# Filter and mixer on one core: the first batch's filter output handed to the mixer within SBUF instead of by way of DRAM

## The chip, the cores and the metric

The kernel runs on one core of a Trainium2 chip. The metric is the device time of one execution in microseconds; the kernel before was timed in three runs. A profile is one execution recorded by the hardware profiler. TensorE (PE) multiplies matrices, VectorE (DVE) and ScalarE (ACT) work elementwise, GpSimd (POOL) does a few sums and issues DMAs, SyncE (SP) only issues DMAs. SBUF is the memory on the core, with 128 partitions; DRAM is the memory beside it.

## The reference, cut to what matters

```python
# x: (8, 3008, 256) f32; filters: (1505, 256) f32; the four mixer weights are float64
def _attn_ref(x, filt_r, filt_i):
    X = np.fft.rfft(x, axis=1)
    Y = X * (filt_r + 1j * filt_i)[None, :, :]
    return np.fft.irfft(Y, n=x.shape[1], axis=1).astype(np.float32)

def _moe_ref(x, w_tok1, w_tok2, w_ch1, w_ch2):
    xt = x.transpose(0, 2, 1)
    h = np.maximum(xt @ w_tok1, 0.0) @ w_tok2      # token mixing, 3008 -> 256 -> 3008
    u = x + h.transpose(0, 2, 1)
    h2 = np.maximum(u @ w_ch1, 0.0) @ w_ch2        # channel mixing, 256 -> 1536 -> 256
    return (u + h2).astype(np.float32)

def reference(**kwargs):
    ...                                            # attention arguments and moe_ arguments parted
    return _moe_ref(x=_attn_ref(**attn_kwargs), **moe_kwargs)
```

The Fourier transform of length 3008 = 47 x 64 is done as matrix products. Its first step runs over 64 points, its second over 47 for each of 32 residues k (`K2`), with the filter's product between; then the steps run backward. The last backward step is not done for itself: it is folded into the token weights (`w1` is turned by `wai_t`), so that the token sums take the results of the second step as they are. These are called g or t4 below. The row for residue k has 4 partitions, 4k to 4k+3, each with 24 values of `a` by 256 channels.

The mixer's weights come as float64. The kernel loads them as 64-bit words in tiles and turns each into a top and a rest in float32 on ScalarE and VectorE: "converting a tile". There are 12 tiles of `w_tok1` and 14 of `w_tok2`, then those of the channel weights. The `w_tok1` tiles and the first six of `w_tok2` also pass through TensorE.

## The kernel before

The main parts that the change and the steps below touch:

```python
BY_PE = 6          # tiles of w_tok2 that pass through TensorE
IN_B = 16          # tiles converted beside the second filter step of the first batch
PARTS = (0, 64, 96, 112)

    t4p = pool("t4p", A // TC4 + 1)                       # 7 buffers of [128, 4, 256] f32
    ...
    def filt_load(c, first):                              # filter rows of residues 2c, 2c + 1
        t, k0 = filts[c % FB], c * KC                     # FB = 3 buffers, KC = 2
        q = nc.gpsimd if first and c != 1 else nc.sync
        for src, i, p0 in (...):                          # first: filt_r and filt_i
            q.dma_start(t[p0:p0 + A, i], raw(src, k0, [[64 * D, A], [D, KC], [1, D]]))
            ...                                           # two more DMAs of mirrored rows
    def filt_double(c):
        nc.scalar.copy(out=t[HALF:P], in_=t[0:HALF])      # line 234
    ...
    def halves(st, n, pair):                              # converting, lines 262 to 270
        nc.scalar.activation(out=top, in_=hi_f, func=AF.Copy, scale=2.0 ** -112)
        yield
        nc.vector.tensor_scalar(...); nc.vector.scalar_tensor_tensor(...)
        yield
        nc.vector.tensor_scalar(...); nc.vector.scalar_tensor_tensor(...)
        yield top, rest
    ...
    def on_chip(stat, top, rest, n, parts):               # the tiles that pass through TensorE
            nc.tensor.matmul(ps[:, 0:n], stat, top, start=True, stop=False)     # line 303
            nc.tensor.matmul(ps[:, 0:n], stat, rest, start=False, stop=True)    # line 304
            for src, dst in parts:
                nc.scalar.copy(out=dst, in_=src(ps))      # line 306
    ...
    def b_unit(k):                                        # second step, forward, and filter
            nc.tensor.matmul(ps, wbs[...], t2, start=True, stop=True)           # line 535
            nc.vector.tensor_tensor(out=p1, in0=ps.to_broadcast([P, 2, D]),
                                    in1=t[:, :, k % KC, :], op=ALU.mult)        # line 543
    def bi_unit(k):                                       # second step, backward
            nc.tensor.matmul(ps[0:KR], wi, p, ...)        # line 560, two per residue
            nc.scalar.copy(out=t3s[c][:, r]..., in_=ps[0:KR]...)                # line 566
            if r == KC - 1:                               # every second residue
                nc.scalar.dma_start(g_d[b, ts(c, KC)]..., t3[:, :, i, :])       # line 571, to DRAM
    ...
    def t4_load(b, c, lo=PARTS[0], hi=P, queue=nc.sync):  # line 611, from DRAM
        queue.dma_start(t4[b, c][lo:hi], rows_of(g_d, b)[lo:hi, ts(c, TC4), :])
    def token_sums(b):                                    # line 617, 48 products
        for a in range(A):
            for t in range(TC):
                nc.tensor.matmul(acc[:, t, :], w1[:, a, ts(t, P)], t4[b, a // TC4][:, a % TC4, :], ...)
    ...
    # the first batch, residue by residue, with tiles converted beside it
                if k == K2 - 5:
                    pause.append(True)                    # begin no new tile loads
                while half < 2 * IN_B * (k + 1) // K2:
                    ...                                   # half a tile's conversion
                if 19 <= k < 25:
                    t4_load(0, k - 19, 0, PARTS[1])       # partitions 0 to 63 back from DRAM
                elif ...                                  # 64 to 95, 96 to 111
        for c in range(A // TC4):
            t4_load(0, c, PARTS[3], P, (nc.sync, nc.gpsimd)[c % 2])   # 112 to 127
        pause.clear()
        ...
        for i in range(IN_B, A // 2 + TC * W2G):          # tiles 16 to 25
            convert()
            if i == A // 2 + BY_PE - 1:                   # after tile 17
                sum_up()
                acc = token_sums(0)
```

The token sums need all of `w1` and all of t4 of the batch; the mixer behind them needs `w2` as well. The other seven batches run through the filter beside the mixer of the batches ahead of them, by way of DRAM.

Of the kernel before, what the change touches and what calls it, by code (L numbers as in the profile page):

```python
# [10 lines left out]
FP32 = mybir.dt.float32  # L11
I64 = mybir.dt.int64
# [7 lines left out]
N1 = 47  # L20
N2 = 64
NF = N // 2 + 1
D = 256
P = 128
K2 = 32
A = 24
# [4 lines left out]
TC4 = 4  # L31
# [3 lines left out]
KC = 2  # L35
WC = 2
DT = 256
TC = DT // P
# [3 lines left out]
DH = D // P  # L42
# [2 lines left out]
MT = 6  # L45
NG = 10
W2G = -(-N2 // NG)
PARTS = (0, 64, 96, 112)
BY_PE = 6
IN_B = 16  # L50
EARLY = 12
GROUPS = ((0,), (1, 2), (3, 4), (5, 6), (7,))

# [74 lines left out]
def kernel(  # L128
# [11 lines left out]
    nc = tc.nc  # L140
# [12 lines left out]
    g_d = nc.dram_tensor("g_tmp", (B, K2, KR, D), FP32, kind="Internal").ap()  # L153
# [3 lines left out]
    def pool(name, bufs, **kw):  # L157
        return ctx.enter_context(tc.tile_pool(name=name, bufs=bufs, **kw))

    glob = pool("glob", 1)  # L160
# [5 lines left out]
    p1p = pool("p1p", 2)  # L166
    p2p = pool("p2p", 1)
    t3p = pool("t3p", 2)
    t4p = pool("t4p", A // TC4 + 1)
    h1p = pool("h1p", 1)  # L170
    up = pool("up", 2)
    hp = pool("hp", 2)
# [21 lines left out]
    wai = glob.tile([P, P], FP32, name="wai")  # L194
# [4 lines left out]
    filts = [glob.tile([P, 2, KC, D], FP32, name="filt%d" % i) for i in range(FB)]  # L199
    w1 = glob.tile([P, A, DT], FP32, name="w1")  # L200

    w2 = glob.tile([P, TC, A * P], FP32, name="w2")

    w2m = [w2[:, t, 0:7 * 256].rearrange("p (s n) -> p s n", s=7) for t in range(2)]
# [8 lines left out]
    def raw(src, row, ap):  # L213
        return bass.AP(tensor=src.tensor, offset=src.offset + row * D, ap=ap)

    def filt_load(c, first):
        t, k0 = filts[c % FB], c * KC


        q = nc.gpsimd if first and c != 1 else nc.sync  # L220
        for src, i, p0 in ((filt_r, 0, 0), (filt_i, 1, 0 if first else HALF)) + (() if first else ((filt_r, 0, HALF),)):
            q.dma_start(t[p0:p0 + A, i], raw(src, k0, [[64 * D, A], [D, KC], [1, D]]))
            lo = p0 + 32
            if k0 == 0:
                q.dma_start(t[lo:lo + A, i, 0, :], raw(src, 32, [[64 * D, A], [1, D]]))
            k = max(k0, 1)

            for j0, n in ((0, 16), (16, A - 1 - 16)):
                q.dma_start(t[lo + j0:lo + j0 + n, i, k - k0:KC, :],
                            raw(src, 64 * (j0 + 1) - k, [[64 * D, n], [-D, k0 + KC - k], [1, D]]))  # L230
# [14 lines left out]

    early = [(up, "u")] * 2 + [(tp, "t")] * 2 + [(vp, "v")] * 2
    late = [(t2p, "t2"), (t3p, "t3")]
    stages = [(t4p, "t4")] * (A // 2) + (early * 3)[0:TC * W2G + DH] + late * 5

    def stage(n):  # L250
        where, tag = stages.pop(0)
        return where.tile([P, n], I64, tag=tag, name="st")

# [41 lines left out]
    ended = [0]  # L295
# [33 lines left out]
    def w2_load(i):  # L329

        t, g = divmod(i, W2G)
        nn = min(NG, N2 - g * NG)
        n = nn * N1

        more = g + 1 < W2G
        st = stage(512)
        nc.gpsimd.dma_start(st[:, 0:n + more], moe_w_tok2[ts(t, P), ds(g * NG * N1, n + more)])
        yield
        dst = w2[:, t].rearrange("p (a h n2) -> p h n2 a", h=2, n2=HALF)[:, :, ds(g * NG, nn), :]

        def some(h, nh, w):
            return (lambda v: bass.AP(tensor=v.tensor, offset=v.offset + h * A, ap=[v.ap[0], [A, nh], [N1, nn], [1, w]]),
                    dst[:, h:h + nh, :, 0:w])

        parts = [some(0, 2, A)] if more else [some(0, 1, A), some(1, 1, A - 1)]
        if i < BY_PE:
            h = halves(st, n + more, spare_pair())
            yield next(h)
            yield next(h)
            on_chip(ident, *next(h), n + more, parts)  # L350
        else:
            yield from rounded(st, n + more, parts, False)
# [23 lines left out]
    def wc2_load(i):  # L376
# [5 lines left out]
        def tile_of(dh):  # L382
# [7 lines left out]
    LAST = ((wc2_load, 0), (wc1_load, 1), (wc1_load, 4), (wc2_load, 1), (wc1_load, 2), (wc2_load, 2), (wc1_load, 5),  # L390
            (wc2_load, 3), (wc2_load, 4), (wc2_load, 5))

    tiles = ([w1_load(i) for i in range(A // 2)] + [w2_load(i) for i in range(TC * W2G)]
             + [wc1_load(c * (DC // 512), False) for c in range(DH)] + [f(i) for f, i in LAST])
# [7 lines left out]
    def sum_up():  # L402
        while behind:
            behind.pop(0)()
# [21 lines left out]
            advance(copy)  # L426
            copied[0] += 1

    begun, pause = [0], []

    def fill(ahead):
        while not pause and begun[0] < len(tiles) and begun[0] < ended[0] + (4 if begun[0] >= len(tiles) - len(LAST) else ahead):
            start()

    def start():
# [5 lines left out]
    xs, ahead = {}, []  # L441
# [22 lines left out]
    def rows_of(t_d, b):  # L464
        return t_d[b].rearrange("k (g a) d -> (k g) a d", a=A)
# [12 lines left out]
    def dft(bs):  # L478
        first = bs[0] == 0
# [40 lines left out]
        t2s, t3s, prods = {}, {}, {}  # L520
# [32 lines left out]
        def bi_unit(k):  # L553


            ps = bank(free_bank() if first else held.pop(0)).rearrange("p (b d) -> p b d", b=2)[:, 0:nb, :]
            parts = prods.pop(k)
            for i, p in enumerate(parts):
                wi = turn_i[:, k // WC % 4, k % WC] if i else wbs[k // WC][:, k % WC, P:]
                nc.tensor.matmul(ps[0:KR], wi, p, start=(i == 0), stop=(i == len(parts) - 1))  # L560
            c, r = divmod(k, KC)
            if r == 0:
                where, tag = (p2p, "p2") if first and c % 3 == 2 else (t3p, "t3")
                t3s[c] = where.tile([KR, KC, nb, D], FP32, tag=tag, name="t3")

            nc.scalar.copy(out=t3s[c][:, r].rearrange("p b (e g i) -> p b g e i", e=DH, i=CW),  # L566
                           in_=ps[0:KR].rearrange("p b (g e i) -> p b g e i", e=DH, i=CW))
            if r == KC - 1:
                t3 = t3s.pop(c)
                for i, b in enumerate(bs):  # L570
                    nc.scalar.dma_start(g_d[b, ts(c, KC)].rearrange("k r d -> r k d"), t3[:, :, i, :])
# [31 lines left out]

    t4 = {}

    def t4_load(b, c, lo=PARTS[0], hi=P, queue=nc.sync):
        if lo == 0:
            t4[b, c] = t4p.tile([P, TC4, D], FP32, tag="t4", name="t4")  # L610
        queue.dma_start(t4[b, c][lo:hi], rows_of(g_d, b)[lo:hi, ts(c, TC4), :])

    def token_sums(b):
        acc = bank(free_bank()).rearrange("p (t d) -> p t d", t=TC)
        for a in range(A):
            for t in range(TC):
                nc.tensor.matmul(acc[:, t, :], w1[:, a, ts(t, P)], t4[b, a // TC4][:, a % TC4, :],  # L617
                                 start=(a == 0 and t == 0), stop=(a == A - 1 and t == TC - 1))
        return acc

# [14 lines left out]
    def u_filter(b, m, dh, ps, first):  # L635
        for q in range(4):
            c, r = divmod(4 * m + q, TC4)
            n = min(P, width(m) - q * P)
            nc.tensor.matmul(ps[:, ds(q * P, n)], t4[b, c][:, r, ts(dh, P)], wai[:, 0:n],  # L639
                             start=(first and q == 0), stop=(not first and q == 3))  # L640

    def u_unit(b, m, h1, ut, dh):
# [287 lines left out]
    with tc.manual_schedule():  # L930
# [6 lines left out]
        for i, _ in enumerate(dft(GROUPS[0])):  # L937
            if i == 0:
                nc.scalar.dma_start(wai_t, wait_d)
            k = i - NXC - 2  # L940

            if i < NXC:
                if i in (1, 3, 5, 7, 9):
                    start()
                if i == NXC - 1:
                    copies()
                    for t, src in ((wa, wa_d), (wai, wai_d), (ident, ident_d)):
                        nc.scalar.dma_start(t, src)
            elif k >= 0:
                if k == K2 - 5:  # L950
                    pause.append(True)
                while half < 2 * IN_B * (k + 1) // K2:
                    if half % 2:
                        convert_end()
                    else:
                        convert_middle()
                    half += 1

                if 19 <= k < 25:
                    t4_load(0, k - 19, 0, PARTS[1])  # L960
                elif 26 <= k < 29:
                    for c in range(2):
                        t4_load(0, 2 * (k - 26) + c, PARTS[1], PARTS[2])
                elif k in (30, 31):
                    for c in range(3):
                        t4_load(0, 3 * (k - 30) + c, PARTS[2], PARTS[3])
        for c in range(A // TC4):
            t4_load(0, c, PARTS[3], P, (nc.sync, nc.gpsimd)[c % 2])
        pause.clear()
        both = wcp.tile([P, 2, JP, 7, P], FP32, tag="wc", name="wc")  # L970

        chan.extend((both[:, 0], both[:, 1]))
        next(second)
        for i in range(IN_B, A // 2 + TC * W2G):
            convert()
            if i == A // 2 + BY_PE - 1:
                sum_up()
                acc = token_sums(0)

        ahead[0](XF, nc.gpsimd)  # L980
        h1s[0] = token_relu(0, acc)
# [61 lines left out]
```

## Time and profile before

| | |
|---|---|
| time, median of three | 2577.78 us (2577.44 to 2580.49) |
| profiled span | 2573.6 us |
| TensorE busy | 2488.4 us, 97% |
| VectorE busy | 1919.8 us, 75% |
| ScalarE, GpSimd busy | 679.8 us, 592.5 us |
| token sums of the first batch | 126.1 to 148.2 us |

The profile's page gives busy time by engine, then the span in 40 slices with a digit for the busy tenths of each. PEld is the loading of weights into TensorE. The chain of waits is found backward from the last instruction: at each step to what released it. A group's line gives the source line, the engine, the operation, `out<-in`, then how often, how long and the idle time ahead. A wait names the instruction that waited, what it waited for, the total in us, how often, and the longest. An fp32 product appears as two matmul records. Of DMAs issued on GpSimd the time from issue to landing is known; of many others only the issue.

### The profile page before, as it was taken

How to read it: one execution, taken by the hardware profiler on the slowest of the kernel's cores; microseconds unless marked ns; L12 is line 12 of the kernel's file. 1: busy time of each engine (PE TensorE's matmuls, PEld its weight loads, DVE VectorE, ACT ScalarE, POOL GpSimd, SP SyncE). 2: the span in 40 equal slices, each digit the busy share in tenths (PEclk: the TensorE clock that was granted, in tenths of full speed). 3: DMA queues.
4: the chain of work that ended last, by engine and by line, in shares of the span. 5: the costliest groups of instructions: out<-in, count | busy, mean ns of one | idle time of the engine just before them, and what ended most of it. 6: DMA issues, size and time to landing. Idle time of an engine off the chain costs nothing.

```text
span 2573.6 us, 32285 instructions
## 1 busy us (share of the span) xinstructions
PE 2488.4 (97%) x11204; PEld 2049.2 (80%) x11204; DVE 1919.8 (75%) x3594; ACT 679.8 (26%) x1342; POOL 592.5 (23%) x1073
## 2 busy tenths in 40 slices
PE   7789999999999999999999999999999999999997
PEld 3467666888888777898888777898888888898887
DVE  7587888567686998756776899856788587757776
ACT  5633222122221222222221222212222122212222
POOL 5563322211211121112121111221211121211222
PEclk8999999999999999999999999999999999999999
DMA  9873434333432333213332343213333222111100
GB/s 221 229 206 127 138 110 136 107 104 106 126 99 79 94 106 89 78 56 117 104 109 86 89 119 96 88 34 110 101 103 95 66 76 71 40 32 37 43 14 20
DMA packets 166432, 248.37 MB, mean 97 GB/s; under 512 B 35300, under 2 KB 112474, under 8 KB 166270
## 3 DMA queue, kind: packets, MB, share of 16 engines
q1 hardware_dynamic: 93006, 150.24, 19.4%
q0 software_dynamic: 33312, 48.47, 7.5%
q10 hardware_dynamic: 39952, 47.61, 5.8%
q8 instruction: 89, 1.46, 0.2%
q14 instruction: 73, 0.60, 0.1%
HBM read 168.96 MB, written 77.22 MB: 96 GB/s over the span
## 4 chain that ended last, share of the span: by engine, by line
PE 74%; DVE 16%; ACT 2%; issue 2%; DMA 1%; ACTq 0%; DVEq 0%; POOL 0%; POOLq 0%; SPq 0%
PE ps_po L774 25%; PE ps_pg L740 15%; PE ps_pg L756 11%; PE ps_b L617 4%; DVE t L718 3%; DVE hh L718 3%; PE ps_acc L661 2%; PE ps_b L661 2%; PE ps_acc L617 2%; DVE u L718 2%; DVE s L718 2%; PE ps_acc L639 2%; PE ps_b L639 2%; PE ps_b L535 1%; PE ps_acc L535 1%
## 5 line engine op out<-in xcount | busy, mean ns | idle before, releaser
L819 POOL DMA_DIRECT2D out_dram<-r x757 | 411.9, 553 | 1753.9 <-ACT t L566 703.2
L718 DVE TENSOR_TENSOR hh<-ps_pg,s 128x512 f32<-128x512 f32 (+3 forms) x864 | 482.3, 586 | 342.7 <-ACT s L743 335.0
L761 ACT ACTIVATE hh<-hh 128x512 f32<-128x512 f32 (+1 forms) x576 | 347.8, 621 | 1199.7 <-DVE hh L718 1199.7
L774 PE MATMUL ps_po<-t,wc 128*128 128x256 f32 (+1 forms) x2304 | 535.7, 375 | 6.4 <-DVE t L718 5.5
L774 PEld LDWEIGHTS ps_po<-t,wc 128*128 128x128 f32 x2304 | 434.2, 190 | 131.4 <-issue 53.2
L740 PE MATMUL ps_pg<-v,wc 128*128 128x256 f32 (+1 forms) x1728 | 413.1, 375 | 2.5 <-DVE v L718 2.4
L774 PE MATMUL ps_po<-hh,wc 128*128 128x256 f32 (+1 forms) x1728 | 412.6, 375 | 0.2 <-ACT hh L761 0.2
L740 PEld LDWEIGHTS ps_pg<-v,wc 128*128 128x128 f32 x1728 | 327.4, 190 | 42.4 <-DVE v L718 5.1
L774 PEld LDWEIGHTS ps_po<-hh,wc 128*128 128x128 f32 x1728 | 327.9, 190 | 38.1 <-ACT hh L761 0.5
L756 PE MATMUL ps_pg<-u,wc 128*128 128x256 f32 (+1 forms) x1152 | 293.5, 377 | 9.0 <-DVE hh L718 8.9
L718 DVE TENSOR_TENSOR t<-t,hh 128x256 f32<-128x256 f32 (+1 forms) x576 | 246.3, 428 | 19.8
L756 PEld LDWEIGHTS ps_pg<-u,wc 128*128 128x128 f32 x1152 | 216.2, 190 | 45.0 <-DVE hh L718 19.9
L718 DVE TENSOR_TENSOR s<-ps_pg,hh 128x512 f32<-128x512 f32 (+1 forms) x288 | 196.0, 681 | 30.0
L718 DVE TENSOR_TENSOR t<-hh 128x512 f32<-128x512 f32 (+1 forms) x288 | 193.3, 671 | 0.6 <-ACT hh L761 0.6
L743 ACT COPY s<-ps_pg 128x256 f32<-128x256 f32 (+1 forms) x288 | 105.9, 368 | 314.3 <-PE ps_pg L740 310.5
L740 PE MATMUL ps_pg<-u,wc 128*128 128x256 f32 (+1 forms) x576 | 169.1, 375 | 2.5 <-DVE hh L718 2.4
L756 PE MATMUL ps_pg<-v,wc 128*128 128x256 f32 (+1 forms) x576 | 168.8, 375 | 0.0
L740 PEld LDWEIGHTS ps_pg<-u,wc 128*128 128x128 f32 x576 | 109.0, 190 | 28.2 <-issue 11.0
L756 PEld LDWEIGHTS ps_pg<-v,wc 128*128 128x128 f32 x576 | 108.7, 190 | 13.1
L718 DVE TENSOR_TENSOR u<-ps_acc,u 128x512 f32<-128x512 f32 (+3 forms) x105 | 61.0, 581 | 76.6 <-PE ps_acc L661 60.1
L617 PE MATMUL ps_b<-t,w 128*128 128x256 f32 x480 | 105.9, 382 | 1.1 <-ACT t L566 1.1
L718 DVE TENSOR_TENSOR u<-ps_b,u 128x256 f32<-128x256 f32 (+3 forms) x105 | 59.4, 566 | 61.1 <-PE ps_b L661 42.4
(132 smaller groups left out, 2526.6 us busy)
## 6 DMA issues: line engine op xcount, KB each, us to landing
w<-w_tmp SPq DMA_DIRECT2D x35, 896.0 KB
g_tmp<-t ACTq DMA_DIRECT2D x128, 192.0 KB
out_dram<-r POOLq DMA_DIRECT2D x698, 32.0 KB, 1.8
z_tmp<-t ACTq DMA_DIRECT2D x84, 256.0 KB
t<-z_tmp SPq DMA_DIRECT2D x112, 192.0 KB
t<-g_tmp SPq DMA_DIRECT2D x42, 512.0 KB
wb<-wbi_t SPq DMA_DIRECT2D x80, 224.0 KB
x<-in_x_dram SPq DMA_DIRECT2D x139, 128.0 KB
```

Source lines behind the costliest of these rows:

```text
L535: nc.tensor.matmul(ps, wbs[k // WC][0:P if first else KR, k % WC, 0:P], t2, start=True, stop=True)
L617: nc.tensor.matmul(acc[:, t, :], w1[:, a, ts(t, P)], t4[b, a // TC4][:, a % TC4, :], start=(a == 0 and t == 0), stop=(a == A - 1 and t == ...
L639: nc.tensor.matmul(ps[:, ds(q * P, n)], t4[b, c][:, r, ts(dh, P)], wai[:, 0:n], start=(first and q == 0), stop=(not first and q == 3))
L661: nc.tensor.matmul(ps[:, ds(j * hw, hw)], h1[:, n, :], w2m[m % 2][:, at, 0:hw], start=(i < 2 and j == 0), stop=(j == len(todo) - 1))
L718: nc.vector.tensor_tensor(out=out, in0=in0, in1=in1, op=op)
L740: nc.tensor.matmul(ps[:, 0:hw], chan[0][:, jp, n, :], mov, start=True, stop=True)
L743: nc.scalar.copy(out=s[:, 0], in_=g[0][:, 0, 0:hw])
L756: nc.tensor.matmul(ps[:, 0:hw], chan[0][:, jp, n, :], mov, start=True, stop=True)
L761: nc.scalar.activation(out=hs, in_=hs, func=AF.Relu)
L774: nc.tensor.matmul(po[i][:, j, 0:hw], chan[1][:, jp, n, :], mov, start=(jp == 0 and first == 1), stop=(jp == JP - 1 and last == 1))
L819: q.dma_start(rows[g, e, :, ds(h * A + 4 * m, n)], blocks[ts(g, CW), h, e, 0:n])
```

## The change

In the first batch the result of each residue, 96 partitions of 1 KB, goes by one DMA within SBUF into the four partitions of the mixer's input that belong to the residue. It is issued by GpSimd. The 16 writes to DRAM of this batch and its 24 reads back fall away. The mixer's input becomes one fixed buffer with seven parts in place of a pool; because it fills from the first residue on, the first seven weight tiles are loaded into the still unused `w2` buffer and the seventh part. 18 tiles in place of 16 are converted beside the filter step, so that all tiles which pass through TensorE lie ahead of the token sums; the pause of the tile loads falls away. To make room on GpSimd, the imaginary filter rows and the `w_tok2` tiles are loaded from SyncE's queue.

```diff
-PARTS = (0, 64, 96, 112)
-IN_B = 16
+IN_B = 18
...
+    t4s = glob.tile([P, A // TC4 + 1, TC4, D], FP32, name="t4")
...
-        q = nc.gpsimd if first and c != 1 else nc.sync
         for src, i, p0 in ((filt_r, 0, 0), (filt_i, 1, 0 if first else HALF)) + (...):
+            q = nc.gpsimd if first and i == 0 and c != 1 else nc.sync
...
-    stages = [(t4p, "t4")] * (A // 2) + (early * 3)[0:TC * W2G + DH] + late * 5
+    first = [w2.rearrange("p t n -> p (t n)")[:, ts(i, 1024)] for i in range(6)]
+    first.append(t4s[:, A // TC4].rearrange("p a d -> p (a d)"))
+    stages = (early * 4)[0:A // 2 - len(first) + TC * W2G + DH] + late * 5
...
-        nc.gpsimd.dma_start(st[:, 0:n + more], moe_w_tok2[ts(t, P), ds(g * NG * N1, n + more)])
+        nc.sync.dma_start(st[:, 0:n + more], moe_w_tok2[ts(t, P), ds(g * NG * N1, n + more)])
...
-            if r == KC - 1:
+            if first:
+                nc.gpsimd.dma_start(t4s[ts(k, 4), 0:A // TC4].rearrange("p c a d -> p (c a) d"), t3s[c][:, r, 0, :])
+            elif r == KC - 1:
                 t3 = t3s.pop(c)
                 for i, b in enumerate(bs):
                     nc.scalar.dma_start(g_d[b, ts(c, KC)].rearrange("k r d -> r k d"), t3[:, :, i, :])
...
-                if k == K2 - 5:
-                    pause.append(True)
...
-                if 19 <= k < 25:
-                    t4_load(0, k - 19, 0, PARTS[1])
-                elif 26 <= k < 29:
...
-        for c in range(A // TC4):
-            t4_load(0, c, PARTS[3], P, (nc.sync, nc.gpsimd)[c % 2])
-        pause.clear()
...
-        for i in range(IN_B, A // 2 + TC * W2G):
+        sum_up()
+        acc = token_sums(0)
+        for _ in range(IN_B, A // 2 + TC * W2G):
             convert()
-            if i == A // 2 + BY_PE - 1:
-                sum_up()
-                acc = token_sums(0)
```

More of the change, by code (lines that the diff above doesn't have):

```diff
@@ L168 @@
     t3p = pool("t3p", 2)
-    t4p = pool("t4p", A // TC4 + 1)
     h1p = pool("h1p", 1)
@@ L247 @@
     late = [(t2p, "t2"), (t3p, "t3")]
-    stages = [(t4p, "t4")] * (A // 2) + (early * 3)[0:TC * W2G + DH] + late * 5
+    first = [w2.rearrange("p t n -> p (t n)")[:, ts(i, 1024)] for i in range(6)]
+    first.append(t4s[:, A // TC4].rearrange("p a d -> p (a d)"))
+    stages = (early * 4)[0:A // 2 - len(first) + TC * W2G + DH] + late * 5
     def stage(n):
+        if first:
+            return first.pop(0).bitcast(I64)
         where, tag = stages.pop(0)
@@ L427, in copies @@
             copied[0] += 1
-    begun, pause = [0], []
+    begun = [0]
     def fill(ahead):
-        while not pause and begun[0] < len(tiles) and begun[0] < ended[0] + (4 if begun[0] >= len(tiles) - len(LAST) else ahead):
+        while begun[0] < len(tiles) and begun[0] < ended[0] + (4 if begun[0] >= len(tiles) - len(LAST) else ahead):
             start()
@@ L567, in bi_unit @@
                            in_=ps[0:KR].rearrange("p b (g e i) -> p b g e i", e=DH, i=CW))
-            if r == KC - 1:
+            if first:
+                nc.gpsimd.dma_start(t4s[ts(k, 4), 0:A // TC4].rearrange("p c a d -> p (c a) d"), t3s[c][:, r, 0, :])
+            elif r == KC - 1:
                 t3 = t3s.pop(c)
@@ L602, in dft, with t4_of, t4_load @@
             yield
[L606 to L611, printed above, removed]
+    def t4_of(b, c):
+        return t4s[:, (b * A // TC4 + c) % (A // TC4 + 1)]
+    def t4_load(b, c):
+        nc.sync.dma_start(t4_of(b, c), rows_of(g_d, b)[:, ts(c, TC4), :])
     def token_sums(b):
@@ L616, in token_sums @@
             for t in range(TC):
-                nc.tensor.matmul(acc[:, t, :], w1[:, a, ts(t, P)], t4[b, a // TC4][:, a % TC4, :],
+                nc.tensor.matmul(acc[:, t, :], w1[:, a, ts(t, P)], t4_of(b, a // TC4)[:, a % TC4, :],
                                  start=(a == 0 and t == 0), stop=(a == A - 1 and t == TC - 1))
@@ L638, in u_filter @@
             n = min(P, width(m) - q * P)
-            nc.tensor.matmul(ps[:, ds(q * P, n)], t4[b, c][:, r, ts(dh, P)], wai[:, 0:n],
+            nc.tensor.matmul(ps[:, ds(q * P, n)], t4_of(b, c)[:, r, ts(dh, P)], wai[:, 0:n],
                              start=(first and q == 0), stop=(not first and q == 3))
@@ L957 @@
                     half += 1
-                if 19 <= k < 25:
-                    t4_load(0, k - 19, 0, PARTS[1])
-                elif 26 <= k < 29:
[L962 to L966, printed above, removed]
-        for c in range(A // TC4):
-            t4_load(0, c, PARTS[3], P, (nc.sync, nc.gpsimd)[c % 2])
-        pause.clear()
         both = wcp.tile([P, 2, JP, 7, P], FP32, tag="wc", name="wc")
```

## The prediction

> **What bounds the kernel now.** I read the slices of the page first, to see where TensorE isn't the bound.
>
> ```profile
> PE   7789999999999999999999999999999999999997
> PEld 3467666888888777898888777898888888898887
> DMA  9873434333432333213332343213333222111100
> ```
>
> A slice is 64 us. From the fourth on TensorE is at 9 and the DMA share at 3 or 4: the mixer, which the change doesn't touch. Only in the first three is TensorE at 7 or 8, with the DMA at 9, 8 and 7. A change to the first batch can win only there. So I cut the first 205 us into stages (columns: stretch, its length, busy us and count for PE, PEld, DVE, ACT, POOL; then clock, DMA share, GB/s).
>
> ```profile
> 36.00:113.00 77.00, 69.08 (x243) 42.86 (x243) 51.07 (x92) 54.78 (x107) 46.23 (x83) 0.97 0.92 227
> 113.00:126.10 13.10, 5.52 (x12) 2.09 (x11) 5.42 (x14) 2.89 (x4) 4.76 (x9) 0.84 0.79 219
> 126.10:148.30 22.20, 22.12 (x97) 18.93 (x95) 20.27 (x41) 5.65 (x10) 10.92 (x21) 0.94 0.60 181
> 148.30:205.00 56.70, 45.83 (x164) 28.94 (x165) 48.58 (x84) 21.62 (x39) 42.66 (x75) 0.97 0.72 215
> ```
>
> Row one is the two filter steps, 8 us of TensorE idle in 77. Row two is the hole between them and the token sums, 7.6 us idle in 13.1. Row three is the token sums, full. Row four is the first mixer blocks, with 11 us idle beside weight conversion on VectorE. Who waits in the first two rows comes from the waits of TensorE and VectorE, 36 to 126 us (total us, times, longest).
>
> ```profile
> PE ps_po L304 <- DVE both L270: 7.6, 2, 7.1
> PE ps_b L560 <- DVE p L543: 7.1, 5, 3.4
> PE ps_acc L560 <- DVE p L543: 0.6, 3, 0.2
> ...
> DVE p L543 <- ACT filt L234: 14.4, 9, 3.5
> DVE both L264 <- ACT both L262: 7.3, 1, 7.3
> DVE p L543 <- DMA filt<-in_filt_i_dram: 6.7, 4, 4.9
> ```
>
> Two causes. The product with the filter (L543) waits for a filter row that has not landed, which costs TensorE 7.1 + 0.6 = 7.7 us. And one weight conversion costs 7.6 us in the hole. The chain of waits says why the hole is there (start, us, what):
>
> ```profile
> 112.60 0.38 ACT t L566
> 113.00 2.12 DMA g_tmp<-t
> ...
> 115.18 0.50 issue
> ...
> 117.43 4.75 DMA st<-in_moe_w_tok_dram
> 122.26 0.38 ACT both L262
> ...
> 124.36 1.94 PE ps_po L304 x2
> 126.30 21.94 PE ps_b L617 x96
> ```
>
> The last result goes to DRAM in 2.12 us. GpSimd then issues three of the reads back, and only behind them, at 117.43, the load of a token weight tile, which waited in the same queue. That tile is converted, TensorE turns it at 124.36, and the token sums start at 126.1. So GpSimd's queue order set the end of the hole, more than the trip through DRAM alone.
>
> [...] filter loads under a 0.92 DMA share take 5.2 us from issue to landing. [...] Nothing in the kernel before writes four partitions[...].
>
> **The change part by part.** The first product starts at 30.63 us, the last ends at 112.6.
>
> 1. The end of the stage. From 112.6 to 126.1 there are 13.5 us. In their place come the copy (0.4), GpSimd's issue (0.55, as its other issues) and the landing. I take 4.2 us for the landing[...]. The sum is 5.2, a gain of **8.3 us**. The weight tile is no longer in this chain: the queue of SyncE loads it, and the pause of the loads is gone.
>
> 2. Two more tiles beside the filter, 18 for 16. On TensorE a tile costs two products of two passes, 0.79 us each for the narrower 471-column tiles, so 2 x 1.58 = **3.2 us** added to the stage. In the kernel before this work lay in the hole that part 1 has counted away. VectorE (51 of 77 us) and ScalarE (55 of 77) have room; ScalarE also loses 16 issues of 0.31 us.
>
> 3. Filter loads on two queues. GpSimd issues six per pair of residues at 0.54 to 0.57 us, 3.3 us, often a weight load of 0.57 ahead, then 5.2 us to land and 1.04 us for ScalarE's doubling: 9.5 us and more. They are asked for four residues ahead, and an undisturbed pair takes 4.3 us (76.92 to 81.22 in the timeline), so there are 8.6 us. That is why TensorE stalls by a few us on some pairs. With three loads each on GpSimd and SyncE, 1.65 us of issue goes, and the weight load too, but two new transfers (1.1 us, each behind ScalarE's copy) come in between on GpSimd. SyncE's loads stand behind 471 KB of weights on their rings. I take half of the 7.7 us: **3.5 us** gained.
>
> 4. DMA load in the stage. Gone: the 16 writes to DRAM, whose queue held 14.4% of all engines from 30 to 112 us, 11.8 us; and 18 of the reads back, 2.7 MB against the 3.1 MB written, so some 10 us more: 22 in all. Added: 32 transfers. [...] if a 1 KB packet costs what it did in the DRAM writes (11.8 us for 3441/16 = 215 packets an engine, 55 ns), some 32 x 6 x 0.055 = 11. With no pause about five 471 KB tiles also come earlier, some 7 us, but those can slip, since they are loaded five ahead. [...] Since prefetch takes up much of it, I put down **1.5 us** lost.
>
> 5. The rest. The token sums (96 products, 22 us), eight tile conversions beside them and the mixer are the same. VectorE's 20.3 of 22.2 us there just fit, and their loads now come earlier. I let the gain pass through to the end undiminished, since after 205 us TensorE is full.
>
> The sum: -8.3 + 3.2 - 3.5 + 1.5 = -7.1 us. From 2577.8 that gives **2570.7**, call it 2570.5.
>
> **The rivals.** [...] it would end 40 to 75 us later, near 2630. For it: [...] a DMA share that is already 0.92. [...] I give it 4%. A milder form, 10 us of new filter stalls, eats the gain: 2578 to 2582, about 10%.
>
> *The bound moves to filter loads on SyncE.* They share rings with weights and tables, which held 60% of the engines' time before, and the loads get one more queue to wait for. Then part 3 is nil or negative and the time is 2574 to 2577. For it: the landing time under load was 5.2 us already. About 20%.
>
> *The gain is larger.* If every filter stall goes, the stage ends at about 112.6 - 7.7 + 3.2 = 108, the token sums start near 113 and 13 us are won: 2565. About 20%.
>
> *The gain is lost later.* From 148 to 205 us TensorE waits for VectorE, so if conversion there hung on loads with a date of their own, an earlier start would only lengthen those waits. Against it: VectorE's work in that stretch, not a landing, is what most of the chain shows, and it moves along. I expect at most 2 us from this.
>
> **Range and chances.** From the sizes of parts 1, 3 and 4 (each about 4 us either way) come 2562 to 2581. Two per cent are 51.6 us, many times what the stage has to give: faster 0.01. Slower by that only in the hard form of the first rival: 0.03. Within: 0.96.
>
> **What the profile after would show.** Part 1: the chain goes from ScalarE's copy through a transfer within SBUF straight to the token sums, with 4 to 7 us from last product to first sum instead of 13.5. Part 2: the tile products all lie ahead of the sums. Part 3: TensorE's wait for the filter product falls from 7.7 to about 4 us. Part 4: the issues list gives the new transfer's landing; under 5 us supports me, over 8 means [...], and filter landings would rise with it. Part 5: from the start of the sums to 205 us the same lengths as before, shifted. The prediction is wrong if the filter stage itself grows by more than 5 us, or if the shift seen at the token sums is not found again at the end.

## The result and the profile after

The changed kernel takes **2612.27 us** (median of four runs, 2606.91 to 2615.64) against 2577.61 before: a ratio of 1.013, with a 95% interval of 1.0108 to 1.0152. It is slower by 34.7 us, where 7 us less were predicted, and the time lies above the range. The profiled execution is the shortest of the four.

The slices of the page, as before:

```profile
PE   6778999999999999999999999999999999999997
DMA  9975343523332333313333233313333222111100
```

The change shows again in the first three slices alone, but TensorE's digits there are lower than before. By stage (stretch, length, busy us and count for PE, PEld, DVE, ACT, POOL; then clock, DMA share, GB/s):

```profile
36.00:145.90 109.90, 83.03 (x254) 48.53 (x252) 55.42 (x102) 56.06 (x111) 43.62 (x72) 0.89 0.93 157
145.90:156.00 10.10, 0.21 (x1) 0.01 (x1) 9.45 (x20) 3.17 (x5) 2.58 (x5) 0.68 1.06 153
156.00:178.90 22.90, 22.83 (x96) 19.51 (x96) 15.26 (x30) 2.39 (x5) 18.12 (x36) 0.92 0.69 183
178.90:235.00 56.10, 45.18 (x170) 29.75 (x171) 43.16 (x78) 22.55 (x40) 31.52 (x57) 1.00 0.61 188
```

The first row is the filter stage. It ends at 145.9 us and not at 112.6: 33.3 us later. The hole behind it is 10.1 us where it was 13.5. So the token sums start 29.9 us later, and the span is 31.5 us longer (2605.1 against 2573.6). The last two rows have nearly the old lengths. The loss arose in the filter stage. Note the last two columns of the first row: the DMA engines are as busy as before (0.93 and 0.92), but they move 157 GB/s in place of 227.

Who waited, 36 to 160 us; two lines for TensorE, then two for GpSimd (30 to 160 us):

```profile
PE ps_b L564 <- DVE p L547: 26.2, 10, 5.4
PE ps_b L623 <- ACT both L266: 9.9, 1, 9.9
```

```profile
POOL t L574 <- ACT t L570: 33.8, 12, 18.1
POOL filt L228 <- DMA t<-t: 31.4, 12, 5.5
```

TensorE's wait for the filter product went from 7.7 us to 26.7 (with 0.5 us on the second bank, as before). TensorE's busy time in the stage also grew, from 69.1 to 83.0 us. By the prediction's count, two tiles more account for 3.2 us of that. The rest are products that take longer in the first few us behind a longer gap (start, us, what, and in brackets the gap):

```profile
60.41 0.79 PE L564 MATMUL ps_b<-p,wb 128*96 128x256 f32 x2 [4.22 <-DVE p L547]
...
61.84 1.91 PE L307 MATMUL ps_po<-both,wai_t 128*128 128x512 f32 x2
...
68.26 1.02 PE L307 MATMUL ps_po<-both,wai_t 128*128 128x512 f32 x2
```

The same product took 1.91 us here and 1.02 us behind the next gap, of only 0.67 us. The granted clock was 0.63 from 60.4 to 65.0 us and 1.00 from 66.0 to 71.9; its mean over the stage is 0.89 against 0.97. GpSimd stood still for 31.4 us with filter loads that waited for a transfer within SBUF to land. In each of these 12 waits the transfer waited for is the eighth DMA before it in GpSimd's queue; of SyncE's waits from 36 to 146 us for a DMA of its own, all 23 are for the eighth before it too. This is the limit of eight that is spoken of below. The list of issues (line by tile: queue, count, KB each, us to landing) from 30 to 146 us and the chain of waits show how long such a transfer takes:

```profile
t<-t POOLq DMA_DIRECT2D x32, 96.0 KB, 10.5
```

```profile
62.94 12.93 DMA t<-t
...
80.01 12.87 DMA t<-t
...
94.64 13.27 DMA t<-t
...
115.59 11.12 DMA t<-t
```

The median is 10.5 us, and these four waits in the chain are over 11. The filter loads of GpSimd went from about 5.2 to about 10 us. So the filter rows came late for two reasons, a late issue and a slow landing; the trace does not divide the 33 us between them.

### The profile page after: what moved, and what is told of

It is laid out like the page before. It is cut to its first block, busy times and chain, and to the rows that moved or that the text cites. A ratio compares the mean times of both kernels' runs of the same rounds, so it can differ in the third digit from the quotient of the medians.

```text
span 2605.1 us, 32283 instructions
## 1 busy us (share of the span) xinstructions
PE 2496.0 (96%) x11204; PEld 2052.7 (79%) x11204; DVE 1918.9 (74%) x3594; ACT 678.0 (26%) x1342; POOL 576.8 (22%) x1042
## 4 chain that ended last, share of the span: by engine, by line
PE 73%; DVE 16%; DMA 5%; issue 3%; ACT 2%; POOL 1%; ACTq 0%; DVEq 0%; SPq 0%; POOLq 0%
PE ps_po L780 25%; PE ps_pg L746 15%; PE ps_pg L762 11%; PE ps_b L623 4%; DVE t L724 3%; DVE hh L724 3%; PE ps_acc L667 2%; PE ps_b L667 2%; PE ps_acc L623 2%; DVE u L724 2%; DMA t<-t 2%; DVE s L724 2%; PE ps_acc L645 2%; PE ps_b L645 2%; PE ps_b L539 1%
## 5 line engine op out<-in xcount | busy, mean ns | idle before, releaser
L762 PEld LDWEIGHTS ps_pg<-u,wc 128*128 128x128 f32 x1152 | 216.0, 190 | 44.5 <-DVE hh L724 19.5
L623 PE MATMUL ps_b<-t,w 128*128 128x256 f32 x480 | 106.6, 384 | 11.0 <-ACT both L266 9.9
L623 PEld LDWEIGHTS ps_b<-t,w 128*128 128x128 f32 x480 | 92.3, 193 | 25.1 <-ACT both L266 10.6
```

What stands on the lines that cost most here:

```text
L623: nc.tensor.matmul(acc[:, t, :], w1[:, a, ts(t, P)], t4_of(b, a // TC4)[:, a % TC4, :], start=(a == 0 and t == 0), stop=(a == A - 1 and t ...
L762: nc.tensor.matmul(ps[:, 0:hw], chan[0][:, jp, n, :], mov, start=True, stop=True)
```

## The experiments

**What to tell apart.** My first theory after the result: a transfer to four neighbouring partitions is slow in itself and takes DMA time from everything beside it. Rivals: the rest of the change slows the stage; the order of GpSimd's queue does it, through the limit of eight; and, within the theory, the place of the four partitions against the number of packets that run at a time. Where the expectations say four engines, the trace shows packets: some four of a transfer to four partitions run at a time, against some 16 of one to 96 (see the transfers by themselves).

### Without the transfers

```diff
-                nc.gpsimd.dma_start(t4s[ts(k, 4), 0:A // TC4]..., t3s[c][:, r, 0, :])
+                pass            # t4s is set to zero once, by GpSimd
```

> The changed kernel without its 32 transfers within SBUF; the mixer's input of the first batch is only set to zero once, so the first batch's output is left out. Theory P (the slow transfers themselves hold up the filter step): the filter stage ends near 110 us in place of 145, time 2560 to 2570. Rival R (the rest of the change, filter rows and weight tiles moved to SyncE's queue and no pause, slows the stage): the stage still ends after 135 us, time over 2590.

Measured: 2553.71 us, ratio to before 0.9906 (0.9892 to 0.9921). That is 6 us under the range expected. TensorE has no wait for the filter product left, and the token sums start at 106.6 us, right behind the last product. The stage by columns as before:

```profile
36.00:105.00 69.00, 68.75 (x250) 44.20 (x250) 54.18 (x98) 56.49 (x109) 21.00 (x39) 0.99 0.84 204
```

TensorE is full, and the DMA share leaves 0.16 x 69 = 11 us of the engines' time free. So the 32 transfers cost 58.6 us (2612.3 - 2553.7), and the rest of the change doesn't slow the stage. Between the profiled executions of the changed kernel and of this run the sums start 49.4 us apart: some 39 us are the longer stage, and 10 the wait for the last transfer. This is no gain to be had: the kernel leaves out the first batch's hand-over.

### The same transfers to 96 partitions

```diff
+                nc.gpsimd.dma_start(t4s[0:KR, k % A // TC4, k % TC4, :], t3s[c][:, r, 0, :])
```

> The same 32 transfers of 96 x 1 KB from GpSimd, but written to 96 partitions each, not to 4; the values land in the wrong places, so the first batch's output is left out. Theory P (destination: 4 partitions[...]): landing falls from 10.5 to 3 to 5.5 us, time 2565 to 2577. Rival Q (any transfer in GpSimd's queue that waits for ScalarE and stands between the filter loads slows them): landing may fall, the time stays over 2595.

Measured: 2561.71 us, ratio 0.9937 (0.9922 to 0.9952), with the token sums from 113.6 us. The time lies 3 us under the range expected, and the landing a little over it (36 to 140 us):

```profile
t<-t POOLq DMA_DIRECT2D x31, 96.0 KB, 6.2
```

Count, bytes, queue and order are those of the changed kernel; only the destination differs, and the 32 transfers cost 8.0 us in place of 58.6. That rules out GpSimd's waits for ScalarE as the cause. It doesn't rule out late landings that hold the queue, since the landing fell too. Some 10 us of the difference are the wait at the end: here the sums start without one, probably as the last row goes to a part that they read later.

### Four partitions, 20 apart

```diff
+                p0 = k if k < 20 else k + 28
+                nc.gpsimd.dma_start(t4s[p0:p0 + 61:20, 0:A // TC4]..., t3s[c][:, r, 0, :])
```

Here and in the run after it the first pair of numbers expected is for the place, the second for the four engines.

> The same transfers to 4 partitions each, but 20 apart in place of neighbours[...]; values land in the wrong places, so the first batch's output is left out. [...] landing 4 to 6 us, time 2565 to 2580. If the split over only four engines[...] is what counts: landing stays 9 to 11 us, time 2600 to 2615.

Measured: 2594.80 us, with a landing of 7.0 us. The run says little: in it one wait of 16.8 us fell on TensorE, because the transfers waited for a weight tile that is loaded into the seventh part of the same buffer (7.3 us in GpSimd's waits). So it was run again with that tile elsewhere:

```diff
-    first.append(t4s[:, A // TC4].rearrange("p a d -> p (a d)"))
```

> Transfers to four partitions 20 apart, as in the run before of that name, but with the weight tile that shared the seventh part of the buffer moved elsewhere, since in that run the transfers waited for it. [...] landing 6 to 7 us, and without that wait a time of 2565 to 2580. Four engines: landing still far above that of 96 partitions, time 2590 or more. First batch's output left out.

Measured: 2587.61 us, ratio 1.0038 (1.0023 to 1.0053), with a landing of 8.2 us; the transfers cost 33.9 us over the run without them. Neither number expected was met: the time lies between the two. Placing the four rows 20 apart gets back 25 of the 58.6 us. Of the 26 us that are left to 96 partitions, 8.1 are a wait of the token sums for the last transfer; whether the rest comes from the place or from the fewer packets at a time, this run doesn't tell.

### The transfers by themselves

A kernel of DMAs only: transfers of 96 x 1 KB of each kind. The first group of numbers expected is for the place.

> No filter and no mixer, only DMAs of 96 x 1 KB from GpSimd with nothing beside them: four in a row, each behind the one before, to four neighbouring partitions, to four partitions 20 apart, to 96 partitions, to DRAM; then eight in flight of each. [...] 5 us alone to neighbours, 2.5 to 3.5 us to partitions 20 apart, about 2 us to 96 partitions and to DRAM. Four engines: the first two alike at 3 to 5 us. Slow only under load: all four about 2 us alone.

Its transfers were reordered and mixed with each other by the scheduler, so it isn't clean; a transfer to neighbours took 5.2 us at the least, 20 apart 3.2, to 96 partitions 1.9, a write to DRAM 2.0. The next one keeps the order, and has loads of 512 KB on SyncE beside the transfers:

> No filter and no mixer. First each kind of transfer of 96 x 1 KB from GpSimd quite alone: [...] 5.2 us to four neighbouring partitions, 3.2 to four partitions 20 apart, 1.9 to 96 partitions. Then 36 loads of 512 KB in rows of 1 KB on SyncE, first by themselves, then beside 24 transfers of each kind. Clogging theory (a transfer to few partitions takes DMA time from everything else[...]): the section with neighbours is 20 us or more longer than the one with 96 partitions. Queue theory (it is only late itself, and holds the later DMAs of its own queue): the loads take the same time within 5 us in all sections.

Measured, quite alone, in this order: neighbours, 20 apart, 96 partitions.

```profile
DMA to landing us min/median/max: 5.5/5.5/5.6
DMA to landing us min/median/max: 3.1/3.1/3.2
DMA to landing us min/median/max: 1.9/1.9/2.0
```

The trace also keeps single packets. A transfer to four partitions, neighbours or 20 apart, is 24 packets of 4 KB, of which about four run at a time; one to 96 partitions is 32, about 16 at a time. So the first two kinds have the same packets and as many at a time, and differ only in their place: a packet takes some 330 ns at the median to neighbours and 159 ns to partitions 20 apart. The limit of eight shows here as well: GpSimd issues eight transfers in 5.2 us, then stands still for 5.5 us until one lands.

Beside the loads the medians are 17.1, 10.4 and 5.9 us. What the transfers do to the loads is read from the queues' lines (packets, MB, share): q1 are the loads, q0 the transfers. First 40 us of the loads alone, then 30 us beside transfers to neighbours, 25 us with four partitions 20 apart, and 15 us with 96 partitions:

```profile
q1 hardware_dynamic: 14055, 13.96, 110.2%
```

```profile
q1 hardware_dynamic: 1605, 1.59, 62.5%
q0 software_dynamic: 1563, 1.38, 53.1%
```

```profile
q1 hardware_dynamic: 3013, 2.99, 69.7%
q0 software_dynamic: 1958, 1.75, 46.1%
```

```profile
q1 hardware_dynamic: 2960, 2.94, 70.1%
q0 software_dynamic: 864, 1.77, 39.1%
```

Alone the loads move 13.96 / 40 = 0.349 MB a us. In 30 us that is 10.47 MB; beside transfers to neighbours they moved 1.59. So 8.88 MB of loads were lost for 1.38 MB of transfers. A transfer has 0.0983 MB, hence 0.633 MB of loads, or 1.81 us of their time. The same sum gives 0.92 us for partitions 20 apart, 0.37 us for 96 partitions, and 0.21 us for writes to DRAM (3.64 MB of loads beside 1.67 MB in 14 us). The loads' own packets show it: one of 1 KB takes 51 ns at the median alone, 180 beside neighbours, 88 beside partitions 20 apart and 56 beside 96 partitions. VectorE waited 90.0 us for the loads of the section with neighbours and 43.4 for those with 96 partitions; since the latter could start some 9 us earlier, that is about 38 us longer. The clogging theory had expected 20 or more, the queue theory under 5.

| destination of 96 x 1 KB | alone, us | takes from the loads, us each | times 32 | longer filter stage, us | cost in the kernel, us |
|---|---|---|---|---|---|
| four neighbours | 5.5 | 1.81 | 58 | 39 | 58.6 |
| four, 20 apart | 3.1 | 0.92 | 29 | 22 | 33.9 |
| 96 partitions | 1.9 | 0.37 | 12 | 7 | 8.0 |

The last two columns are over the run without transfers; the first of them, from the profiled executions, leaves out the wait at the end. They follow, in order and roughly in size, the DMA time that a quite different program measures. That 58 and 58.6 agree is chance in part, since some 10 us of the 58.6 are the wait for the last transfer. In the kernel the other loads slow down too: their packets of 1,792 bytes took 113 ns on average in the stage before, 124 without transfers and 171 with them. So the cause is shown as far as the destination goes, and so is it that transfers to few partitions take time from other DMAs. How much of the stage's 39 us comes from that, and how much from late landings that hold GpSimd's queue, is not shown.

### Four DMAs in place of one

In place of one DMA to four partitions, four DMAs of 24 rows to one partition each. If the place is the cost, the transfers to neighbours take as much from the loads in four DMAs as in one:

```diff
+            for g in range(4):
+                nc.gpsimd.dma_start(tgt["onebyone"][ds(4 * k + g, 1)]..., s[ts(g, A)])     # neighbours
+                nc.gpsimd.dma_start(tgt["apart"][ds(p0 + 20 * g, 1)]..., s[ts(g, A)])      # 20 apart
```

> No filter and no mixer: 36 loads of 512 KB in rows of 1 KB on SyncE beside 24 residues' worth of transfers (96 x 1 KB each): by one DMA to four neighbouring partitions; by four DMAs of 24 KB, each to one partition[...]; the same with the four partitions 20 apart[...]; and without transfers at both ends. [...] If the split over four engines is the cost, both kinds of four DMAs[...] add 10 to 15 us.

60 us of the first kind, and 50 us of the second:

```profile
q1 hardware_dynamic: 10574, 10.50, 97.9%
q0 software_dynamic: 1533, 1.16, 13.3%
```

```profile
q1 hardware_dynamic: 12473, 12.39, 97.1%
q0 software_dynamic: 1686, 1.29, 11.7%
```

Loads lost per transferred MB: (20.94 - 10.50) / 1.16 = 9.0 for neighbours and (17.45 - 12.39) / 1.29 = 3.9 for partitions 20 apart. With one DMA they were 6.4 and 3.3. Each DMA of 24 KB is 12 packets of 2 KB, all begun within 0.11 us, where one DMA had about four running at a time. So more packets at a time didn't help here; partitions apart did. The sections' lengths, of which the expectation spoke, can't be compared, because here GpSimd ended last with its four times as many DMAs. The number of DMAs and the size of the packets changed as well, so the number at a time alone is not tested.

### Fewer DMAs on GpSimd

```diff
-                q.dma_start(t[lo + j0:lo + j0 + n, i, k - k0:KC, :],
+                nc.sync.dma_start(t[lo + j0:lo + j0 + n, i, k - k0:KC, :],
```

> The changed kernel, complete, with the two mirrored filter loads of each pair moved from GpSimd to SyncE, so that GpSimd issues 3 DMAs per pair of residues and not 5. In the compiled program each DMA of a queue waits for the eighth before it to land; with 10.3 us to land and 5 per pair that makes 6.4 us a pair, with 3 per pair 3.9. Queue theory: the stage goes to about 4.5 to 5.5 us a pair, time 2575 to 2590, unless SyncE's own eight (8 per pair now) bind. Clogging theory: stays over 2600.

Measured: 2624.93 us, ratio 1.018 (1.0162 to 1.0198). GpSimd now waits for no landing in the stage, only for ScalarE, and yet the stage ends at 154.7 us, later still. Waits of GpSimd and of ScalarE, 30 to 150 us:

```profile
POOL t L574 <- ACT t L570: 107.0, 22, 22.9
```

```profile
ACT filt L233 <- DMA filt<-in_filt_i_dram: 53.3, 10, 8.4
```

Now the rows that come by SyncE are late, and that queue too waits for its own earlier DMAs (20.6 us ahead of the mirrored filter loads, for weight tiles and other filter rows). The transfers still take 9.7 us; the last one took 17.9, and the token sums started only at 172.7 us. The reservation made beforehand applies: SyncE's own limit of eight may bind, so this run alone does not decide between the theories. It does show that moving these loads to SyncE's queue doesn't cure the stall.

### By way of DRAM, with the rest of the change

```diff
+            if r == KC - 1:                 # writes to g_d from ScalarE, as before
+                if 19 <= k < 25:
+                    t4_load(0, k - 19, 0, PARTS[1])
+        ...                                 # and the other parts as before; no pause
```

> Everything of the change but the transfers within SBUF: the first batch goes by way of DRAM as before (writes on ScalarE's queue, reads in four parts), with filter rows and weight tiles on SyncE, 18 tiles, no pause. If the transfers are the only harm and the rest is the gain: token sums start at 112 to 116 us, time 2560 to 2567. If the gain of the rest needed the DRAM trip gone: 2570 to 2580.

Measured: 2581.50 us, ratio 1.0015 (1.0009 to 1.0022): slower than before, and above the range expected. The last two DMAs of the chain, with their time on it:

```profile
119.23 7.34 DMA g_tmp<-t
...
128.90 5.35 DMA t<-g_tmp
```

The last write takes 7.3 us, behind weight tiles that are loaded ahead, where it took 2.12 with the pause. The hole is 15.5 us. SyncE's filter rows also waited 18.8 us for writes to DRAM to land. So the pause of the kernel before seems to have had a use: it kept the weight loads away from the last trip. A version with a pause for the last three residues, and the early reads on GpSimd:

```diff
+                if k == K2 - 3:
+                    pause.append(True)
+                    t4_load(0, k - 19, 0, PARTS[1], nc.gpsimd)
```

> The first batch by way of DRAM with the rest of the change, as in the run before of that kind, but with a pause of the tile loads for the last three residues, so that the last write is not behind weight loads, and the early reads back on GpSimd's queue, so that SyncE's filter rows don't wait for writes. Last write about 2 to 3 us, read 3.5, hole about 7 us; stage without SyncE's waits ends at 109 to 113: token sums at 116 to 120 us, time 2566 to 2572. If the stage's stalls stay: 2574 to 2580.

Measured: 2573.41 us, ratio 0.998 (0.9972 to 0.9988), between the two ranges.

```profile
117.67 2.42 DMA g_tmp<-t
...
120.13 3.67 DMA t<-g_tmp
```

The hole is 7.4 us, as expected, but the stage's last product is at 116.6 us with 8.4 us of waits for the filter product left, so the token sums start at 123.9. It is faster than both kernels: 4 us under the kernel before. Over the run without transfers, the way by DRAM costs 27.8 us without the pause and 19.7 with it, where the way within SBUF costs 58.6.

### Single parts, on the kernel before

```diff
-        q = nc.gpsimd if first and c != 1 else nc.sync
+            q = nc.gpsimd if first and i == 0 and c != 1 else nc.sync
```

> The kernel before with one part of the change alone: the imaginary filter rows from SyncE's queue. By the prediction's third step TensorE's 7.7 us of waiting for the filter product falls by half: time 2572 to 2576. Since all 7.7 us were gone in the run without transfers it may be up to 7 us: 2570. Rival: the seven to eight DMAs a pair on SyncE and ScalarE[...] hold the filter rows up: 2578 to 2590.

Measured: 2574.75 us, ratio 0.9987 (0.998 to 0.9995). TensorE's wait for the filter product is 6.2 + 1.5 = 7.7 us, what it was. SyncE's filter rows waited 17.2 us for earlier writes to DRAM. The time lies in the range expected, but by luck: the small gain is not from where I had looked for it, and its source stays open.

```diff
-            t4_load(0, c, PARTS[3], P, (nc.sync, nc.gpsimd)[c % 2])
+            t4_load(0, c, PARTS[3], P, (nc.sync, nc.scalar)[c % 2])
-                if k == K2 - 5:
-                    pause.append(True)
```

> The kernel before with the three last reads of GpSimd issued by ScalarE and the pause of the tile loads gone, so that the weight tile isn't queued behind them. If that queue order sets the hole of 13.5 us, the token sums start at 119 to 121 us in place of 126.1 and the time is 2571 to 2573. If the earlier tile loads slow the last write and reads instead (7.3 and 5.3 us in the run by way of DRAM without the pause), nothing is won: 2576 to 2582.

Measured: 2573.27 us, ratio 0.9982 (0.9974 to 0.9991); token sums from 121.8 us, near what was expected, 4.3 us earlier than before. The last write took 4.3 us, 2.2 more than before, and ScalarE, which issued the reads, converted only after them. So GpSimd's queue order and the pause together were part of the hole, and the slower write takes some of the gain back; the two edits were not tried apart.

## Why the prediction was wrong

1. **The end of the stage.** I put the hole at 5.2 us, with a landing of 4.2, an estimate with no measured transfer of this kind behind it. It is 10.1, since the last transfer landed in 9.9 (issued at 145.7 us, landed at 155.6). The direction was right, the gain 3.4 us and not 8.3. The trace names a weight conversion as the releaser of the token sums; the program shows no need for it, and the landing fits. In the run with partitions 20 apart and the weight tile elsewhere the trace names the transfer itself, with 8.1 us.
2. **Two more tiles.** As far as it can be told, right: all tile products lie ahead of the sums.
3. **Filter loads on two queues.** The mechanism was not shown. Alone it left TensorE's wait at 7.7 us, and with the rest of the change and the DRAM trip it was 8.4. In the run without transfers the wait was gone, but there the DRAM trip was gone too. The 60% that SyncE's queue is said to hold before is that of 36 to 76 us; from 30 to 113 us it is 52%. The limit of eight was missing from this step, though the kernel before has it too: from 36 to 113 us all 12 of GpSimd's waits for a DMA of its own are for the eighth before. It makes a late landing hold the next loads, whatever the issue costs.
4. **DMA load in the stage.** This is the step that failed, in two places. I had the right term, the 32 transfers, and sized it too small, with no measured transfer to four partitions. The packet time of the DRAM writes, 55 ns, makes 11 us in all; beside loads 1.81 us each and 58 in all were measured. In the kernel the DMA share makes 0.84 x 70.6 = 59 us of DMA time in the stage without transfers and 0.93 x 110.1 = 102 with them, so 43 us for the 32, an estimate from these two shares. Then I set the balance at 1.5 us lost, on the ground that prefetch would take up much of it. But the stage had only 11 us of DMA time free even without the transfers. TensorE's wait for the filter product went up by 19 us. And products slowed behind the longer gaps: from 36 us to the end of these two stages TensorE has 254 records each, which take 70.4 us without transfers and 83.2 with them. Of slower products the prediction had nothing. The stage grew by 33 us, where it had set 5 as the sign that it was wrong.
5. **The rest.** Right. The sums came 29.9 us later and the end 31.5; without transfers the sums came 19.5 us earlier and the end 21.5.

The rival that I gave 4%, transfers that hold up the other DMAs for 40 to 75 us, is the nearest to what happened. I sized it as all or nothing, 40 to 75 us late or 10, and left nothing for 33. What it rested on was an estimate that no trace showed; the runs show the cost by destination, but not how a transfer holds the others. Its sign in the profile, landings over 8 us and filter landings rising with them, is what the trace shows: 10.5 us, and filter landings from 5.2 to about 10.

What stays open: how the transfers hold the others, engine by engine, as the trace doesn't name single engines; how the loss divides between that and the held queue; what the place and the number of packets at a time each add; and whether SyncE's limit of eight or the clogging bound the run with fewer DMAs on GpSimd.

## What to carry to other kernels

When a transfer saves a trip through DRAM, ask where it lands: here four neighbouring partitions cost the other DMAs more than six times the bytes, and a stage with little DMA time to spare paid for it. Measure such a transfer beside a stream of loads, by what the loads lose, and not by its own landing time. And read DMA share together with GB/s: the same share at 157 in place of 227 GB/s was here the sign of transfers to few partitions.

## What was not expected of the hardware

- 96 x 1 KB to four neighbouring partitions takes 5.5 us alone and 17 us beside loads, and costs those loads 1.81 us; a write of the same rows to DRAM costs them 0.21 us. Even with the reads back, going by way of DRAM was the cheaper road (2573 and 2582 us against 2612).
- The loads' rate fell from 0.349 to 0.053 MB a us beside these transfers, with both queues together reported as busy as before (116% and 110%).
- Matmuls in the first few us behind a gap of 4.2 us ran at about half speed (1.91 against 1.02 us), so that the stall cost more than its length.
